# P.V, division and transposes of x of the first batch three steps, not five, behind a slot's mask

## The chip, the core and the metric

The kernel runs on one core of a Trainium2 chip. The metric is the time of one execution in microseconds (us) on the device; the median of several executions counts. The core's engines work in parallel, each through its own list of instructions in order: TensorE (PE) does matmuls and transposes and loads weights (PEld), VectorE (DVE), ScalarE (ACT) and GpSimd (POOL) work elementwise, and SyncE (SP) issues the DMAs of this kernel. Semaphores make an instruction wait for what it needs. [...]

## What is computed

Attention with a threshold over 4 batches, 8 heads, 576 positions and 64 dimensions a head; then two gated feed-forward layers over the 2304 tokens.

```python
scores = scale * np.matmul(q, k.transpose(0, 1, 3, 2))
thresh = np.max(scores, axis=-1, keepdims=True) - tau
scores = np.where(scores >= thresh, scores, -1000000000.0)
scores = scores - np.max(scores, axis=-1, keepdims=True)
attn = np.exp(scores)
attn = attn / (np.sum(attn, axis=-1, keepdims=True) + 1e-09)
return np.matmul(attn, v).astype(np.float32)
...
gate = 1.0 / (1.0 + np.exp(-(x @ w_gate)))
val = x @ w_val
return (gate * val @ w_out).astype(np.float32)      # layer one: 512 -> 1536 -> 512
...
a = x @ w1
b = x @ w2
h = a * b @ w3
return (h @ w_out).astype(np.float32)               # layer two: 512 -> 1024 -> 512
```

## The kernel before

**Attention.** Heads are taken in pairs: 16 pairs, four to a batch (`NPAIR` = 4). The queries of a pair fall into nine row blocks of 128, called slots (`NSL` = 9): four for each head, and one, the tail, that holds the last 64 rows of both. So there are `G` = 144 slots, 36 to a batch. Slot g passes through these steps:

- `s_mm` (PE): the score products into one of two PSUM buffers, `ps_s0` for even g and `ps_s1` for odd; products are split into a high and a low part, so that a slot takes two or three passes (`ka` and `ylz`, for the tail `xk` and `yk`);
- `s_max` (DVE, tile `nm`, line 321) and `s_exp` (ACT, tile `e`, line 327);
- `s_mask` (DVE, line 336): exponentials below the threshold become 0, and the row sum is taken. It frees the PSUM buffer for slot g+2;
- `s_hi` (ACT, line 344), and `s_lo` (ACT line 355 and POOL line 358, or DVE line 360): P as two 16-bit halves, tile `h16`, shown as `h`;
- `s_tr`: a transposing DMA, issued on SP (line 364), writes `pt`, of which there are five buffers;
- `pv` (PE): 14 small matmuls (28 for a tail) of `pt` with `vh`, `vl` and `vsh`, into `u`, and for the tail into a corner of a score buffer (`ut`).

After a pair's nine slots come `x_norm` (DVE: division by the row sums, tiles `xn` and `xt`), `x_pe` (PE: transposes, tiles `ps_x` and a corner of `ps_s`) and `x_act` (ACT, lines 417 and 419: into the x of the batch, `XR0` to `XR3`). A pair is a quarter of the 512 features of x, chunk c of four. The next pair's q, k and v are loaded, transposed, split and scaled meanwhile (`t_pe` to `v_split`, by the table `ahead`).

**Work between the slots.** `filler` puts other matmuls into the program twice a step. At first it is `merge_gen`, which multiplies w3 by w_out (tiles `woh`, `wol`); then `l1_gen`, layer one. Layer one runs batch by batch: an `h_unit` gives two units of 12 matmuls (`ps_h`, 288 columns), an `o_unit` nine (`ps_o`). It needs x of its batch split into high and low halves (`xh` on ACT, `xl` on POOL or DVE, line 467 and 468), chunk by chunk, and `ready(b)` holds it until `xdone` counts the batch. Its weights arrive by DMA and are cast and split for batch 0 on DVE, ACT and POOL (lines 449 to 468). `budget(g)` sets how much of it a call takes: until g = 44 one unit a call, later so much that the batches' work is spread evenly up to the time when the next batch is ready. Layer two follows all attention.

**Order.** The loop at line 825 runs over steps g and traces the parts in a fixed order: mask of g, maximum of g+1, scores of g+2, `s_tr` of g-2, and P.V of g-5 (`LAG` = 5); `x_norm` falls into step 9n+5, `x_pe` and `x_act` into the two after it. This order is only a priority: the scheduler takes, engine by engine, what is ready in its own reckoning of time. So the order of the built program differs from the order of the text.

```python
done = divmod(g - LAG, NSL)
...
if done[1] == 2 and done[0] > 0:
    x_act(done[0] - 1)
    if done[0] % NPAIR == 0:
        xdone[0] = done[0] // NPAIR
filler(g, 0)
...
if 0 <= g - LAG < G:
    pv(g - LAG, g)
```

Of the kernel before, what the change touches and what calls it, by code (L numbers as in the profile page):

```python
# [22 lines left out]
def kernel(  # L23
# [25 lines left out]
    NPAIR = H // 2  # L49
# [243 lines left out]
    NSL = 2 * NC + 1  # L293
# [91 lines left out]
    def x_norm(pr):  # L385
        p = prep[pr]
        rs = ap_.tile([P, NSL], F32, tag="rs", name="rs", bufs=1)
        nc.vector.tensor_scalar(rs, p["sum"], 1e-9, None, op0=ALU.add)
        nc.vector.reciprocal(rs, rs)
        xn = ap_.tile([P, NC, 2, D], F32, tag="xn", name="xn")  # L390
        xt = ap_.tile([P, 2, D], F32, tag="xt", name="xt")
        nc.vector.tensor_tensor(
            xn.rearrange("p c h d -> p h c d"), p["u"],
            rs[:, 0:2 * NC].rearrange("p (h c x) -> p h c x", h=2, x=1).to_broadcast([P, 2, NC, D]),
            op=ALU.mult,
        )
        nc.vector.tensor_scalar(
            xt, p["ut"][:, 0:P].rearrange("p (x d) -> p x d", x=2),
            rs[:, 2 * NC:NSL], None, op0=ALU.mult,
        )  # L400
        p.update(xn=xn, xt=xt)
# [77 lines left out]
    def flush(keep):  # L479
        while len(defer) > keep:  # L480
            defer.pop(0)()
# [257 lines left out]
    xdone = [0]  # L739
# [6 lines left out]
    LAG = 5  # L746
    G = NP * NSL
    spent = [0]

    def run(gen, ns):  # L750
        while gen is not None and ns > 0:
            t = next(gen, "end")
            flush(1)
            if t == "end":
                return None
            if t is None:
                return gen
            ns -= t
            spent[0] += t
        return gen  # L760
# [64 lines left out]
    for g in range(G + LAG + 3):  # L825
        pr, s = divmod(g, NSL)
        steps = ahead[s] if pr + 1 < NP else ([],) * 5
        done = divmod(g - LAG, NSL)
        if g < G:
            s_mask(g)  # L830
        if g + 1 < G:
            s_max(g + 1)
        if g < G:
            s_hi(g)
        if g + 1 < G:
            s_exp(g + 1)
        if g + 2 < G:
            s_mm(g + 2)
        for f in steps[3]:
            f(pr + 1, g)  # L840
        if done[1] == 0 and done[0] > 0:
            x_norm(done[0] - 1)
        if g < G and g % 2 == 0 or g // (NPAIR * NSL) == 0:
            s_lo(g)
        if 0 < g <= G and not ((g - 1) % 2 == 0 or (g - 1) // (NPAIR * NSL) == 0):
            s_lo(g - 1)
        if 2 <= g < G + 2:
            s_tr(g - 2)
        for f in steps[0]:
            f(pr + 1)  # L850
        for f in steps[1]:
            f(pr + 1)
        if done[1] == 2 and done[0] > 0:
            x_act(done[0] - 1)
            if done[0] % NPAIR == 0:
                xdone[0] = done[0] // NPAIR
        filler(g, 0)
        for f in steps[2]:
            if isinstance(f, str):
                if pr + 2 < NP:  # L860
                    load(src[f], pr + 2, f)
            else:
                f(pr + 1)
        if 0 <= g - LAG < G:
            pv(g - LAG, g)
        for f in steps[4]:
            f(pr + 1)
        if done[1] == 1 and done[0] > 0:
            x_pe(done[0] - 1, g)
        filler(g, 1)  # L870
    order.close()
    actx.close()
# [282 lines left out]
```

## Time and profile before

| | |
|---|---|
| Runs | 1141.19, 1147.88, 1150.70 us; median 1147.88 |
| The profiled execution | 1143.68 us, its span 1141.9 us |
| Busy, of the span | PE 90%, weight loads 85%, DVE 69%, POOL 58%, ACT 55% |
| Mean granted clock of PE | 0.965 |
| Matmuls | 8256 |
| DMA | 324738 packets, 245.34 MB |

A busy share is an average over stretches with different limits, so the views below are cut by stretch: 143 us is about the end of the merge, 209.5 us the place where layer one of batch 0 gets going, 353 us about slot 72, 392 us about slot 82, and 711 us the last P.V. The releaser in brackets is what ended the idle time of the engine ahead of the row. Helpers record several kinds of matmul under one line (63), so tiles tell them apart.

### The profile page before, as it was taken

The numbers are of one execution on the slowest core, as the hardware profiler recorded it, in microseconds if no ns is written. First come the engines' busy times: TensorE is split into PE (matmuls) and PEld (weight loads), VectorE is DVE, ScalarE is ACT, GpSimd is POOL, SyncE is SP. The second block draws the span as 40 slices with busy tenths as digits, with TensorE's granted clock in tenths as the row PEclk, the third lists the DMA queues.
The fourth block names the chain that finished last, engine by engine and source line by source line (L and its number), as shares of the span: only waits on it lengthen the run. The fifth ranks groups of instructions, "written<-read, shape, count | busy, mean of one in ns | idle before, by whom it ended". The sixth has DMA issues, their size and how long they took to land.

```text
span 1141.9 us, 23155 instructions
## 1 busy us (share of the span) xinstructions
PE 1024.9 (90%) x8256; PEld 967.5 (85%) x8256; DVE 788.6 (69%) x1485; ACT 626.1 (55%) x1306; POOL 657.9 (58%) x593
## 2 busy tenths in 40 slices
PE   2598956899898799999899999999789999999997
PEld 2477745799888799999799999989789989998996
DVE  6988588988797766677757754698886653662740
ACT  4877797878587666566656665545542311231210
POOL 2655384688685866766665685577862441460420
PEclk9999968899899899999899999999989999999999
DMA  7999999999998898977876764898767857866824
GB/s 211 260 277 208 221 214 176 268 272 264 275 259 211 193 209 177 182 172 174 183 178 148 159 142 113 292 371 298 257 202 232 253 174 228 266 194 188 289 77 129
DMA packets 324738, 245.34 MB, mean 215 GB/s; under 512 B 225552, under 2 KB 254224, under 8 KB 324624
## 3 DMA queue, kind: packets, MB, share of 16 engines
q1 hardware_dynamic: 324624, 243.87, 82.2%
q8 instruction: 65, 1.06, 0.4%
q14 instruction: 49, 0.40, 0.1%
HBM read 141.56 MB, written 35.13 MB: 155 GB/s over the span
## 4 chain that ended last, share of the span: by engine, by line
PE 60%; DMA 13%; DVE 10%; POOL 5%; issue 5%; ACT 4%; SPq 3%; DVEq 0%; POOLq 0%; ACTq 0%
PE ps_h L63 16%; PE ps_ab L63 15%; PE ps_o L63 9%; PE ps_y L63 8%; PE ps_s L63 6%; DMA pt<-h 4%; PE u L63 3%; DMA vnat<-in_v_dram 1%; PE ps L63 1%; DMA sc_c<-wc 1%; DVE e L336 1%; DVE ps_c L449 1%; DVE nm L321 1%; DMA XR<-in_moe_w_out_dram 1%; DMA wms<-sc_m 1%
## 5 line engine op out<-in xcount | busy, mean ns | idle before, releaser
L358 POOL TENSOR_TENSOR h<-e,h 128x576 f16<-128x576 f32 x90 | 117.0, 1302 | 50.8 <-ACT e L355 35.0
L327 ACT ACTIVATE e<-ps_s,nm 128x576 f32<-128x576 f32 x144 | 106.2, 738 | 59.8 <-DVE nm L321 57.5
L63 PEld LDWEIGHTS <-pt 128*128 128x128 f16 x2240 | 83.7, 102 | 61.8 <-DMA pt<-h 50.2
L321 DVE TENSOR_REDUCE nm<-ps_s 128x1 f32<-128x576 f32 x144 | 107.2, 751 | 40.1 <-PE ps_s L63 26.9
L63 PE MATMUL ps_o<-gvl,oh 128*128 128x288 f32 x384 | 118.8, 312 | 9.5 <-DVE XR L695 5.6
L63 PE MATMUL ps_h<-xl,gh 128*128 128x288 f32 x384 | 120.9, 315 | 6.6 <-ACT gh L467 4.4
L336 DVE SCALAR_TENSOR_TENSOR e<-ps_s,th,e 128x576 f32<-128x576 f32 x144 | 116.8, 812 | 14.1 <-ACT th L328 10.3
L63 PE MATMUL ps_h<-xl,vh 128*128 128x288 f32 x384 | 117.6, 306 | 3.5 <-ACT th L664 1.8
L63 PE MATMUL ps_h<-xh,gl 128*128 128x288 f32 x384 | 115.4, 300 | 4.6 <-DVE gl L468 4.6
L63 PE MATMUL ps_o<-gvh,ol 128*128 128x288 f32 x384 | 114.8, 299 | 0.5 <-DVE ol L468 0.5
L63 PE MATMUL ps_h<-xh,vl 128*128 128x288 f32 x384 | 114.8, 299 | 0.4 <-DVE vl L468 0.4
L63 PE MATMUL ps_h<-xh,gh 128*128 128x288 f32 x384 | 114.9, 299 | 0.0
L63 PE MATMUL ps_o<-gvh,oh 128*128 128x288 f32 x384 | 114.3, 299 | 0.0
L344 ACT ACTIVATE h<-e 128x576 f16<-128x576 f32 x144 | 97.3, 678 | 30.9 <-DVE e L336 25.5
L63 PE MATMUL ps_h<-xh,vh 128*128 128x288 f32 x384 | 114.2, 298 | 0.0
L63 PE MATMUL u<-vh,pt 128*128 128x64 f16 x640 | 63.6, 201 | 45.2 <-DMA pt<-h 44.4
L468 POOL TENSOR_TENSOR gvl<-gr,gvh 128x288 fp32r<-128x288 f32 x82 | 74.0, 902 | 47.1 <-ACT gvh L467 42.3
L63 PE MATMUL ps_y<-wm,abh 128*128 128x512 f32 x288 | 91.7, 391 | 0.2 <-DMA wm<-sc_n 0.2
L63 PE MATMUL ps_s<-ka,qa 128*128 128x288 f32 x256 | 64.4, 339 | 27.4 <-DVE e L336 15.4
L1023 POOL TENSOR_TENSOR v<-u,u 128x384 f32<-128x384 f32 x24 | 25.5, 1068 | 107.7 <-DVE u L1023 56.6
L63 PEld LDWEIGHTS ps_o<-gvl,oh 128*128 128x128 f32 x384 | 73.7, 193 | 11.2 <-DVE XR L695 6.1
L669 DVE SCALAR_TENSOR_TENSOR gr<-th,ps_h 128x288 f32<-128x288 f32 x96 | 43.2, 450 | 56.2 <-PE ps_h L63 34.8
(199 smaller groups left out, 3284.5 us busy)
## 6 DMA issues: line engine op xcount, KB each, us to landing
wc<-sc_c SPq DMA_DIRECT2D x168, 256.0 KB, 3.3
sc_c<-wc SPq DMA_DIRECT2D x56, 256.0 KB, 4.6
wm<-sc_n SPq DMA_DIRECT2D x24, 512.0 KB, 3.5
XR<-in_moe_w_out_dram SPq DMA_DIRECT2D x20, 512.0 KB, 4.8
ka<-xk SPq DMA_DIRECT2D x64, 144.0 KB, 3.3
wg<-sc_g SPq DMA_DIRECT2D x36, 256.0 KB, 3.5
wv<-sc_v SPq DMA_DIRECT2D x36, 256.0 KB, 3.2
wo<-sc_o SPq DMA_DIRECT2D x36, 256.0 KB, 3.5
```

Of the source, the lines that this page charges most:

```text
L63: nc.tensor.matmul(out_, lhsT, rhs, start=first, stop=last)
L321: nc.vector.tensor_reduce(nm, x["ps"], axis=AX.X, op=ALU.max, negate=True)
L327: nc.scalar.activation(e, x["ps"], AF.Exp, bias=x["nm"])
L336: nc.vector.scalar_tensor_tensor(x["e"], x["ps"], x["th"], x["e"], op0=ALU.is_ge, op1=ALU.mult, accum_out=prep[pr]["sum"][:, s:s + 1],)
L344: nc.scalar.activation(x["h16"][:, 0:S], x["e"], AF.Copy, scale=PSC)
L358: nc.gpsimd.tensor_tensor(lo, e, hi, op=ALU.subtract)
L449: first = nc.vector.tensor_scalar(t0, hw, 3, 0xC0000000, op0=ALU.logical_shift_left, op1=ALU.bitwise_or)
L468: (lo_eng or nc.gpsimd).tensor_tensor(lo, x, hi.bitcast(F32), op=ALU.subtract)
L669: nc.vector.scalar_tensor_tensor(r, t, 1.0, pss["v"][:, 0:HS], op0=ALU.add, op1=ALU.mult)
L1023: eng.tensor_tensor(sv[w][nm], x, y, op=ALU.add)
```

## The change

A function `lag(g)` gives three for the slots of the first batch and five for the others. A step now takes P.V of each slot whose lag ends with it: step 38 takes that of slot 35, steps 39 and 40 none, step 41 that of slot 36. `x_norm`, `x_pe` and `x_act` come one, two and three steps behind the P.V of a pair's last slot; for batch 0 they move two steps ahead, and `xdone` becomes 1 at step 41 and no longer at step 43.

```diff
--- before.py
+++ after.py
@@ -747,6 +747,10 @@
     G = NP * NSL
     spent = [0]
 
+    def lag(g):
+
+        return LAG - 2 if g < NPAIR * NSL else LAG
+
     def run(gen, ns):
         while gen is not None and ns > 0:
             t = next(gen, "end")
@@ -825,7 +829,8 @@
     for g in range(G + LAG + 3):
         pr, s = divmod(g, NSL)
         steps = ahead[s] if pr + 1 < NP else ([],) * 5
-        done = divmod(g - LAG, NSL)
+        due = [x for x in range(max(0, g - LAG), min(g, G)) if x + lag(x) == g]
+        past = {g - x - lag(x): x // NSL for x in range(NSL - 1, min(g, G), NSL)}
         if g < G:
             s_mask(g)
         if g + 1 < G:
@@ -838,8 +843,8 @@
             s_mm(g + 2)
         for f in steps[3]:
             f(pr + 1, g)
-        if done[1] == 0 and done[0] > 0:
-            x_norm(done[0] - 1)
+        if 1 in past:
+            x_norm(past[1])
         if g < G and g % 2 == 0 or g // (NPAIR * NSL) == 0:
             s_lo(g)
         if 0 < g <= G and not ((g - 1) % 2 == 0 or (g - 1) // (NPAIR * NSL) == 0):
@@ -850,10 +855,10 @@
             f(pr + 1)
         for f in steps[1]:
             f(pr + 1)
-        if done[1] == 2 and done[0] > 0:
-            x_act(done[0] - 1)
-            if done[0] % NPAIR == 0:
-                xdone[0] = done[0] // NPAIR
+        if 3 in past:
+            x_act(past[3])
+            if past[3] % NPAIR == NPAIR - 1:
+                xdone[0] = past[3] // NPAIR + 1
         filler(g, 0)
         for f in steps[2]:
             if isinstance(f, str):
@@ -861,12 +866,12 @@
                     load(src[f], pr + 2, f)
             else:
                 f(pr + 1)
-        if 0 <= g - LAG < G:
-            pv(g - LAG, g)
+        for x in due:
+            pv(x, g)
         for f in steps[4]:
             f(pr + 1)
-        if done[1] == 1 and done[0] > 0:
-            x_pe(done[0] - 1, g)
+        if 2 in past:
+            x_pe(past[2], g)
         filler(g, 1)
     order.close()
     actx.close()
```

The names below are those of the two built programs, cut by lines left out. On ACT, at the end of batch 0's x: `XR_78` is x of batch 0, L419 the copy of the tail of its last pair, L327 and L328 the exponential and threshold of slots 43 and 44 (before) and 42 and 43 (after). Before:

```order
L327 ACTIVATE e<-ps_s_92,nm 128x576
L328 ACTIVATE th<-nm,ntau 128x1
L327 ACTIVATE e<-ps_s_91,nm 128x576
L328 ACTIVATE th<-nm,ntau 128x1
L419 ACTIVATE XR_78<-ps_s_91,vi 64x64 x2
L284 ACTIVATE vh<-vnat 128x640
L467 ACTIVATE xh<-XR_78 128x576
L344 ACTIVATE h_2649<-e 128x576
```

After:

```order
L327 ACTIVATE e<-ps_s_91,nm 128x576
L328 ACTIVATE th<-nm,ntau 128x1
L419 ACTIVATE XR_78<-ps_s_91,vi 64x64 x2
L327 ACTIVATE e<-ps_s_92,nm 128x576
L467 ACTIVATE xh<-XR_78 128x576
L328 ACTIVATE th<-nm,ntau 128x1
L344 ACTIVATE h_2671<-e 128x576
L284 ACTIVATE vh<-vnat 128x640
```

The copy stood behind the exponential of slot 44 and stands behind that of slot 42 now; the split of the last chunk (`xh`) follows one exponential later, ahead of `vh`.

On PE, where layer one of batch 0 goes on with the last chunk (`ps_h`): `xk,qbd` and `yk,qbd` are the scores of slot 44, `ka` and `ylz` those of the slots behind it, `u<-..,pt` rows P.V. Before:

```order
L63 MATMUL ps_s_91<-xk,qbd_93 128x288 x4
L63 MATMUL ps_s_91<-yk,qbd_93 128x288 x2
L411 MATMUL ps_s_91<-ident,xt 128x128
...
L63 MATMUL u<-vh,pt 128x64
...
L63 MATMUL ps_s_92<-ka,qa 128x288 x2
L63 MATMUL ps_s_92<-ylz_98,qa 128x288 x2
...
L63 MATMUL ps_s_91<-ka,qa 128x288 x2
L63 MATMUL ps_s_91<-ylz_98,qa 128x288 x2
...
L63 MATMUL u<-vsh,pt 128x64
L63 MATMUL ps_h<-xl,gh 128x288
L63 MATMUL ps_h<-xh,gl 128x288
```

After:

```order
L63 MATMUL ps_s_91<-xk,qbd_93 128x288 x4
L63 MATMUL ps_s_91<-yk,qbd_93 128x288 x2
L63 MATMUL ps_h<-xl,gh 128x288
L63 MATMUL ps_h<-xh,gl 128x288
L63 MATMUL ps_h<-xh,gh 128x288
L63 MATMUL ps_h<-xl,vh 128x288
L63 MATMUL ps_h<-xh,vl 128x288
L63 MATMUL ps_h<-xh,vh 128x288
L63 MATMUL ps_s_92<-ka,qa 128x288 x2
L63 MATMUL ps_s_92<-ylz_98,qa 128x288 x2
```

P.V of slots 39 to 41 and the scores of slots 45 and 46 stood between slot 44's scores and layer one; now layer one follows slot 44's scores at once.

On PE, at the scores of slot 34 (`ps_s_91<-ka` and `ylz_99`) and P.V of slot 29 (`u<-vh,pt` to `u<-vsh,pt`). Before:

```order
L63 MATMUL ps_s_91<-ka,qa 128x288 x2
L63 MATMUL ps_s_91<-ylz_99,qa 128x288 x2
L156 MATMUL ps_t<-ident,km 128x128 x4
L63 LDWEIGHTS vb
L63 MATMUL ps_s_91<-identb,vb 128x128
L63 LDWEIGHTS pt
L63 MATMUL u<-vh,pt 128x64
```

After:

```order
L411 MATMUL ps_s_92<-ident,xt 128x128
L63 LDWEIGHTS pt
L63 MATMUL u<-vh,pt 128x64
...
L63 MATMUL u<-vsh,pt 128x64
L63 MATMUL ps_s_91<-ka,qa 128x288 x2
L63 MATMUL ps_s_91<-ylz_99,qa 128x288 x2
```

The P.V stood behind the scores, and stands ahead of them now.

## Rows read from the trace of the kernel before

**Rows 1.** Page: the span of the profiled execution

```profile
span 1141.9 us, 23155 instructions
```

**Rows 2.** Busy time of each engine by stretch; first line names the columns

```profile
core 0: us, PE busy (x) PEld busy (x) DVE busy (x) ACT busy (x) POOL busy (x), PEclk, DMA share, GB/s
...
143.00:199.30 56.30, 32.77 (x351) 28.01 (x352) 45.82 (x99) 48.63 (x99) 37.41 (x31) 0.76 0.95 194
199.30:209.50 10.20, 7.09 (x62) 6.41 (x61) 8.27 (x15) 7.57 (x16) 3.11 (x4) 0.50 0.99 191
209.50:353.00 143.50, 133.39 (x1247) 128.50 (x1247) 125.37 (x246) 106.04 (x221) 112.64 (x96) 0.98 1.10 266
353.00:392.00 39.00, 30.77 (x313) 29.20 (x312) 29.04 (x60) 28.29 (x63) 29.55 (x26) 0.91 0.89 208
392.00:711.00 319.00, 312.77 (x3106) 303.70 (x3105) 211.33 (x431) 197.28 (x420) 209.65 (x197) 0.98 0.76 168
```

**Rows 3.** The same for line 336 alone (masks, two records a slot)

```profile
162.00:199.30 37.30, 11.51 (x28) 0.82 0.94 174
...
209.50:353.00 143.50, 22.13 (x54) 0.98 1.10 266
353.00:392.00 39.00, 8.28 (x21) 0.91 0.89 208
```

**Rows 4.** Timeline of PE (start us, us, instruction, idle before it), 199 to 213

```profile
199.63 1.16 PE L63 MATMUL ps_s<-xk,qbd 128*128 128x288 f32 x4
...
204.70 0.23 PE L63 MATMUL u<-vh,pt 128*128 128x64 f16 x1 [3.11 <-DMA pt<-h]
...
209.22 0.51 PE L63 MATMUL ps_h<-xl,gh 128*128 128x288 f32 x1
...
211.28 0.29 PE L63 MATMUL ps_h<-xh,gl 128*128 128x288 f32 x1
...
212.61 0.29 PE L63 MATMUL ps_h<-xh,gh 128*128 128x288 f32 x1
```

**Rows 5.** Timeline of ACT, same columns, 202 to 206

```profile
202.43 0.74 ACT L327 ACTIVATE e<-ps_s,nm 128x576 f32<-128x576 f32 x1 [1.75 <-DVE nm L321]
...
204.06 0.62 ACT L419 ACTIVATE XR<-ps_s,vi 64x64 f32<-64x64 f32 x2
...
205.34 0.67 ACT L467 ACTIVATE xh<-XR 128x576 fp32r<-128x576 f32 x1
```

**Rows 6.** Timeline of DVE, same columns, 203 to 208

```profile
203.20 0.82 DVE L279 TENSOR_TENSOR vnat<-vnat,ps_s 128x640 f32<-128x640 f32 x1
...
207.46 0.75 DVE L468 TENSOR_TENSOR xl<-XR,xh 128x576 fp32r<-128x576 f32 x1
```

**Rows 7.** Waits of PE, 209.5 to 353: who for whom, us, times, longest

```profile
PE ps_o L63 <- DVE XR L695: 5.6, 3, 3.9
PE ps_h L63 <- ACT th L664: 1.8, 2, 1.2
```

**Rows 8.** Waits of PE, 353 to 392

```profile
PE u L63 <- DMA pt<-h: 4.3, 1, 4.3
```

**Rows 9.** Timeline of PE, three pairs of score product and P.V

```profile
97.12 0.77 PE L63 MATMUL ps_s<-xk,qbd 128*128 128x288 f32 x4
...
99.16 0.19 PE L63 MATMUL u<-vh,pt 128*128 128x64 f16 x1
...
171.94 0.52 PE L63 MATMUL ps_s<-ka,qa 128*128 128x288 f32 x2
...
174.09 0.20 PE L63 MATMUL u<-vh,pt 128*128 128x64 f16 x1 [0.87 <-DMA pt<-h]
...
176.53 0.54 PE L63 MATMUL ps_s<-ka,qa 128*128 128x288 f32 x2
...
177.95 0.20 PE L63 MATMUL u<-vh,pt 128*128 128x64 f16 x1 [0.62 <-DMA pt<-h]
```

**Rows 10.** Waits of PE, 60 to 209.5

```profile
PE u L63 <- DMA pt<-h: 24.1, 15, 3.1
```

## Prediction

> **What bounds the kernel now.** I read the table of busy time by stretch first, because the share of the whole span hides that the stretches have different limits. From 392 us to 711 us PE is busy for 312.77 of 319 us, and from 209.5 to 353 us for 133.39 of 143.5 us; from 143 to 199.3 us it is busy for only 32.77 of 56.3 us, at a granted clock of 0.76 [rows 2]. So from 209.5 us the kernel is a stream of matmuls with attention threaded through it, and ahead of that it is attention by itself, waiting on chains between engines. I then read the pace of attention from the masks alone: 14 slots in 37.3 us (2.66 us each) from 162 to 199.3 us, where PE has little besides attention; 27 slots in 143.5 us (5.3 us each) where layer one of batch 0 fills PE; and 10.5 slots in 39 us (3.7 us each) from 353 to 392 us, where that work runs out ahead of batch 1's [rows 3]. The waits of the first stretch say what PE waits for there: 15 times for the transposed P to land, 24.1 us in all [rows 10].
>
> The point where the first stretch turns into the second is layer one of batch 0 getting its last quarter of x. The first 18 matmuls ran early on the other three quarters; the rest resumes at 209.22 us [rows 4], 0.3 us ahead of the clock's rise from 0.50 at 209.5 us [rows 2]. That is the place the change touches most.
>
> **The change part by part.** Nothing is added or removed: as many matmuls, divisions, copies and DMAs as before. P.V, division and transposes of x of slots 0 to 35 are traced two steps earlier, and batch 0 counts as done at step 41, not 43. The scheduler then orders the engines anew.
>
> P.V itself hardly moves. In the order of PE I counted how many slots' scores stand ahead of each P.V: for slots 8 to 38 it is slot plus 4.5 on average in both kernels. Its readiness, not its place in the program, set its position already. Single ones move: those of slots 12, 29 and 31 now stand ahead of a score product that used to precede them. By the times of before, PE would be held from 97.12 to 99.16, from 171.94 to 174.09 and from 176.53 to 177.95 us [rows 9]: 2.0, 2.2 and 1.4, in sum 5.6 us at most. Others (13, 14, 21 to 24) move the other way. At least nothing is lost, since PE has 23.5 us of idle time there from 143 to 199.3 us [rows 2]; I take a quarter, **+1.3 us**, nearer to that idle time. If that cover is gone, all 5.6 us count. Behind a waiting P.V on PE stands the next score product, and for that wait the maximum, the exponential and the mask of its slot.
>
> The end of x moves. Now: the copy of the tail of x at 204.06, the split's high half at 205.34 [rows 5], its low half from 207.46 to 208.21 [rows 6], then P.V of slots 39 to 41 and two scores, then layer one at 209.22 [rows 4]. After: on ACT the copy stands ahead of slot 43's exponential and the high half right behind it. That exponential ran at 202.43 for 0.74 us [rows 5], so the high half ends about 203.9; the low half stands behind the product on `vnat`, which ends at 204.02 [rows 6], and ends about 204.8. On PE the resumed matmuls now stand right behind slot 44's scores (199.63 [rows 4]) and ahead of P.V 39. So layer one resumes at about 204.8, 4.4 us earlier. What is that worth? Not the 3.11 us in which PE waited for P.V 39 until 204.70 [rows 4]: the new first instruction is ready no sooner. What remains is that PE worked at half clock until 209.5 [rows 2]. If the clock rises with layer one, as it did at 209.5, the 4.7 us from 204.8 hold 2.4 us more work; if it does not, nothing. I take **-2.4 us**, the row's own coincidence.
>
> The rest of layer one's work is shifted, not shortened. A matmul of 288 columns takes (212.61-211.28)/10 = 0.133 us [rows 4]; two steps with two filler calls each give four units of 12, or 6.4 us of PE earlier. In the new order 396 of layer one's matmuls stand ahead of slot 58's scores, where 312 stood; 756 ahead of slot 72's, where 708 stood; and 819 ahead of slot 81's in both, since batch 1 still becomes ready at step 79. The lead is given back. So two slots without layer one leave the first stretch and two join the stretch from 353 us. Out go 2 x 2.66 = 5.3 us, in come 2 x 2.66 to 2 x 3.7 = 7.4 us: 0 to +2.1 us. I take **+1.0 us**, the middle, since the slots at 3.7 us carried layer one's remainder.
>
> Last, layer one's own waits. Spread over two more slots, its accumulations into x (5.6 us of waiting in 3 places) and its tanh (1.8 us) may be awaited less [rows 7]. Bounds 0 and -7.4 us; I take **-3.0 us**, under half, because the order of DVE that makes the longest (3.9 us) is not undone. The DMA queue of SP issues the same transfers; its transposes stand within two or three rows of where they stood, so I cost them at nothing, hidden by the 5.3 us a slot has in that stretch; without that cover the price is one more wait as that of 4.3 us [rows 8].
>
> Sum: +1.3 - 2.4 + 1.0 - 3.0 = -3.1 us. The profiled execution took 1143.68 us (span 1141.9 [rows 1] and 1.8 us around it); it would become 1140.6. The median of the runs is 4.2 us above it, 1147.88, and becomes 1144.8, or 1145 in round figures.
>
> **The rivals.** *Nothing moves.* P.V keeps its distance, layer one is level at slot 81, and PE is full from there; the four terms cancel. For it speaks that the order of PE is nearly the same from about slot 86 on; against it, the half clock just ahead of 209.5. Time: 1147.9.
>
> *The lead is kept.* If attention, rid of layer one in the stretch from 353 us, runs its slots there at 2.66 us as it did ahead of 199.3, two slots (5.3 us) are saved outright, with the 2.4 us of clock and the 7.4 us of waits: -15.1 us, 1132.8. For it: that pace was reached once [rows 3]. Against: PE waited 4.3 us there for one P.V [rows 8], so latency and not PE held it. It decides from about 12 us in all.
>
> *P.V holds back the scores.* A P.V on PE that comes two steps sooner waits for its transposed P, and the next scores wait behind it; then batch 0 slows down. One wait costs 24.1/15 = 1.6 us [rows 10]; from eight more such waits (12.8 us) the kernel is slower by over 1%, about 1160.5. For it: three such pairs are in the order. Against: three make 5.6 us, not 12.8, and the mean distance is unchanged. [...]
>
> **How the numbers follow.** Chances: my forecast 0.46, nothing moves 0.25, the lead kept 0.17, P.V holding back 0.12. About 1% is what a measurement of this kernel can tell from no change: 1136.4 to 1159.4 us. The forecast's own bounds are -2.4-7.4 = -9.8 (1138) and +5.6+2.1 = +7.7 (1155.6). With half of the two outer rivals taken in, the range is 1134 to 1156. Faster by over 1%: 0.18, the kept lead and a trace of the forecast; slower: 0.11; within 1%: 0.71.
>
> **What would show it.** In the profile of the changed kernel: the first resumed `ps_h` matmul ahead of P.V 39, some 4 us before the same slot's place now; the clock at 1.00 a few us sooner after it; 5 us a slot or more while layer one runs; a longer stretch of slots at 3 to 3.7 us ahead of 392 us. PE's waits for the landing of transposed P up to 209.5 us should stay near 24 us. If they pass 36 us, I am wrong on the slow side; if the stretch ahead of slot 83 runs at 2.7 us a slot, on the fast side. A shift of the whole profile after 711 us would be none of these.

## The result, and the profile after

The changed kernel takes 1153.85 us (median of 16 runs, 1146.35 to 1159.07), the kernel before on the same chip 1146.92 us (16 runs, 1141.19 to 1152.58). The ratio is 1.0065, interval 1.0045 to 1.0085: **7 us slower**, where 3 us faster was forecast. The profiled execution of the changed kernel is the fastest of all its runs (1146.35 us), so that the readings below are repeated on two more profiles of each order of instructions.

Its span on the page:

```profile
span 1144.6 us, 23156 instructions
```

The same table by stretch as [rows 2] (PE, PEld, DVE, ACT, POOL busy, granted clock, DMA share, GB/s), cut where the clock rises. The granted clock is TensorE's, as a share of full; the clock records of both kernels' profiles hold only 1.00 and 0.50 (half), and a stretch shows the mean:

```profile
143.00:196.50 53.50, 31.46 (x313) 26.79 (x313) 43.49 (x84) 44.12 (x89) 35.86 (x31) 0.68 0.93 189
196.50:209.50 13.00, 10.42 (x108) 9.76 (x108) 11.59 (x27) 11.13 (x26) 4.86 (x5) 1.00 0.88 202
209.50:353.00 143.50, 137.18 (x1321) 131.68 (x1320) 126.98 (x251) 108.19 (x225) 113.15 (x98) 1.00 1.12 266
353.00:392.00 39.00, 26.90 (x261) 23.78 (x260) 29.41 (x56) 27.27 (x57) 28.94 (x25) 0.82 0.99 211
392.00:711.00 319.00, 308.89 (x3040) 299.56 (x3040) 210.59 (x428) 194.50 (x416) 205.78 (x193) 0.98 0.77 169
```

Against [rows 2], PE does more from 209.5 to 353 us (137.18 us busy for 133.39), and less in the two stretches behind: 26.90 for 30.77, and 308.89 for 312.77. The masks of line 336 (two records a slot; answers to [rows 3]) tell the same of attention:

```profile
162.00:199.30 37.30, 9.40 (x23) 0.72 0.90 173
209.50:353.00 143.50, 22.73 (x56) 1.00 1.12 266
353.00:392.00 39.00, 8.13 (x20) 0.82 0.99 211
```

The timeline of PE where layer one resumes, answering [rows 4]; P.V of slot 39 now stands behind it:

```profile
205.39 0.40 PE L63 MATMUL ps_h<-xl,gh 128*128 128x288 f32 x1 [0.34 <-DVE xl L468]
...
210.01 0.21 PE L63 MATMUL u<-vh,pt 128*128 128x64 f16 x1
```

And the waits of PE (who for whom, us, times, longest): from 60 to 209.5 us (answers [rows 10]), from 209.5 to 353 (the four longest; [rows 7]), from 353 to 395 ([rows 8]) and from 395 to 545 us:

```profile
PE u L63 <- DMA pt<-h: 21.4, 13, 3.9
...
PE ps_x L407 <- DVE XR L693: 1.6, 1, 1.6
PE ps_h L63 <- DVE yk L239: 1.1, 1, 1.1
PE ps_h L63 <- ACT vh L467: 1.0, 1, 1.0
PE ps_s L63 <- DVE e L336: 0.9, 1, 0.9
...
PE ps_s L63 <- DVE e L336: 9.2, 4, 5.1
...
PE ps_o L63 <- DVE XR L693: 2.2, 1, 2.2
PE ps_h L63 <- DVE XR L695: 1.6, 1, 1.6
```

In the kernel before, the masks from 353 to 395 us:

```profile
PE ps_s L63 <- DVE e L336: 3.7, 3, 1.6
```

So the waits for transposed P did not grow, of the 5.6 us for accumulations into x 0.4 us are left, and two new ones stand further down: 9.2 us for masks where 3.7 stood, and 2.2 us for a copy into x in a place where the kernel before waits for nothing.

**Where the time goes, stretch by stretch.** Stretches cut by the clock on the wall compare different work, so I cut by work. Each matmul counts with the median interval from its start to the next one's, over those at full clock with no idle time between (by its operands, from the profiles of both kernels). Both kernels then hold the same 952.4 us of work, and a mark says how much of it PE has begun. The table gives the time between marks, mean and range over three profiles: of the kernel before (first profile, before_again, before_red) and of the changed one (first profile, after_again, after_red). Early marks cut off slightly different sets of matmuls; behind 262 the orders of PE differ by some dozens of rows, and from mark 308 (445 to 449 us) on the list of every engine is the same in both kernels.

| Work marks | time in before | before, us | changed, us | difference |
|---|---|---|---|---|
| 0 to 90 | to 172 | 168.8 (167.0 to 172.0) | 167.0 (166.3 to 167.5) | -1.8 |
| 90 to 120 | to 225 | 53.9 (53.1 to 55.1) | 50.4 (49.8 to 50.9) | -3.5 |
| 120 to 240 | to 362 | 136.2 (135.7 to 136.9) | 133.4 (132.8 to 134.5) | -2.7 |
| 240 to 262 | to 397 | 36.0 (35.0 to 36.5) | 42.3 (42.0 to 42.7) | +6.3 |
| 262 to 400 | to 541 | 143.8 (142.4 to 144.7) | 150.1 (148.4 to 153.3) | +6.3 |
| 400 to 430 | to 583 | 40.3 (38.6 to 41.3) | 42.0 (41.3 to 42.9) | +1.6 |
| 430 to end | to 1134 | 551.2 (550.6 to 551.7) | 551.6 (549.8 to 553.0) | +0.4 |

The sum is +6.7 us, close to what the medians say; the three profiles of the changed kernel by themselves give +1.5, +7.2 and +11.3. So 8.0 us are won up to mark 240, and 14.2 lost from there to 430. From 90 to 262, where layer one of batch 0 runs, win and loss cancel.

### The profile page after: what moved, and what is told of

It is laid out like the page before. It is cut to its first block, busy times and chain, and to the rows that moved or that the text cites. A ratio compares the mean times of both kernels' runs of the same rounds, so it can differ in the third digit from the quotient of the medians.

```text
span 1144.6 us, 23156 instructions
## 1 busy us (share of the span) xinstructions
PE 1026.5 (90%) x8256; PEld 965.8 (84%) x8256; DVE 790.5 (69%) x1485; ACT 625.7 (55%) x1306; POOL 657.4 (57%) x593
## 4 chain that ended last, share of the span: by engine, by line
PE 58%; DVE 14%; DMA 11%; ACT 6%; issue 6%; POOL 4%; SPq 1%; DVEq 0%; POOLq 0%; ACTq 0%
PE ps_h L63 16%; PE ps_ab L63 15%; PE ps_y L63 8%; PE ps_o L63 7%; PE ps_s L63 5%; DMA pt<-h 4%; PE ps L63 3%; PE u L63 3%; DVE ps_c L449 2%; DVE nm L321 2%; DVE e L336 2%; DVE t L455 1%; ACT h L344 1%; DMA wms<-sc_m 1%; DMA vnat<-in_v_dram 1%
## 5 line engine op out<-in xcount | busy, mean ns | idle before, releaser
L327 ACT ACTIVATE e<-ps_s,nm 128x576 f32<-128x576 f32 x144 | 106.5, 739 | 57.0 <-DVE nm L321 52.9
L321 DVE TENSOR_REDUCE nm<-ps_s 128x1 f32<-128x576 f32 x144 | 107.5, 751 | 40.3 <-PE ps_s L63 23.7
L336 DVE SCALAR_TENSOR_TENSOR e<-ps_s,th,e 128x576 f32<-128x576 f32 x144 | 116.6, 812 | 15.4 <-ACT th L328 11.5
L63 PEld LDWEIGHTS ps_h<-xl,gh 128*128 128x128 f32 x384 | 73.8, 192 | 12.1 <-ACT gh L467 4.9
L468 POOL TENSOR_TENSOR ol<-wo,oh 128x512 fp32r<-128x512 f32 x41 | 56.7, 1390 | 45.4 <-ACT oh L467 45.4
```

The lines of the kernel that those rows point to most:

```text
L63: nc.tensor.matmul(out_, lhsT, rhs, start=first, stop=last)
L321: nc.vector.tensor_reduce(nm, x["ps"], axis=AX.X, op=ALU.max, negate=True)
L327: nc.scalar.activation(e, x["ps"], AF.Exp, bias=x["nm"])
L336: nc.vector.scalar_tensor_tensor(x["e"], x["ps"], x["th"], x["e"], op0=ALU.is_ge, op1=ALU.mult, accum_out=prep[pr]["sum"][:, s:s + 1],)
L468: (lo_eng or nc.gpsimd).tensor_tensor(lo, x, hi.bitcast(F32), op=ALU.subtract)
```

## The experiments

All ratios are to the kernel before, on the same chip in the same session (its medians there 1145.0 to 1146.2 us). The right half is the table above for the one profile of each run: difference to the mean of the kernel before, by stretch and in sum, in us.

| Run | ratio, 95% interval | 0-90 | 90-120 | 120-240 | 240-262 | 262-400 | 400-430 | rest | sum |
|---|---|---|---|---|---|---|---|---|---|
| last_pair | 1.0010 (0.9986 to 1.0035) | +0.8 | -2.8 | -2.5 | +6.3 | +0.8 | -0.8 | -0.5 | +1.3 |
| first_pairs | 1.0089 (1.0061 to 1.0116) | -1.2 | +2.4 | +3.7 | +2.4 | +2.8 | -0.3 | -1.4 | +8.4 |
| two3 | 0.9990 (0.9971 to 1.0009) | -3.0 | -1.8 | -3.6 | +3.0 | +7.3 | -0.9 | +0.9 | +2.1 |
| after_again | 1.0065 (1.0041 to 1.0089) | -2.6 | -3.3 | -1.7 | +6.8 | +4.8 | +1.4 | +1.8 | +7.2 |
| before_again | 1.0008 (0.9987 to 1.0028) | +3.2 | -0.4 | -0.5 | +0.5 | +0.9 | +0.8 | +0.5 | +5.1 |
| before_spread8 | 0.9981 (0.9963 to 1.0000) | +0.3 | -0.8 | +6.0 | -6.3 | +0.3 | -4.9 | +2.8 | -2.6 |
| after_spread8 | 0.9987 (0.9971 to 1.0004) | +0.3 | -3.1 | +13.0 | -3.5 | +0.3 | -5.6 | -3.2 | -1.9 |
| after_spread4 | 1.0097 (1.0072 to 1.0123) | -0.7 | -3.3 | +5.2 | +2.1 | +2.3 | -3.0 | +14.8 | +17.4 |
| last_pair_spread8 | 1.0015 (0.9993 to 1.0036) | +1.1 | -4.3 | +11.5 | -6.0 | +1.0 | -4.3 | +4.3 | +3.3 |
| two3_spread8 | 0.9987 (0.9970 to 1.0005) | -1.3 | -2.8 | +4.0 | -6.6 | +3.6 | -0.3 | +1.3 | -2.0 |
| vmax_dep0 | 1.0047 (1.0021 to 1.0074) | -0.4 | -4.2 | -2.6 | +6.1 | +3.5 | +2.0 | +0.5 | +4.9 |
| late_start | 1.0068 (1.0046 to 1.0090) | +2.7 | -0.2 | +3.2 | -1.4 | +1.7 | -0.4 | +0.5 | +6.1 |
| hold_start | 1.0129 (1.0107 to 1.0152) | -0.6 | -1.6 | +6.1 | +1.4 | +0.5 | +2.9 | 0.0 | +8.7 |
| pair0 | 1.0107 (1.0085 to 1.0129) | -2.6 | +0.2 | +11.1 | +2.7 | -1.5 | +0.5 | +0.9 | +11.4 |
| after_red | 1.0066 (1.0041 to 1.0092) | -1.4 | -3.0 | -3.4 | +6.2 | +9.6 | +2.5 | +0.9 | +11.3 |
| hold_start_red | 1.0069 (1.0046 to 1.0093) | +1.9 | -1.5 | +5.4 | +2.0 | +1.4 | +0.5 | +0.5 | +10.2 |
| before_red | 1.0001 (0.9981 to 1.0021) | -1.3 | +1.2 | -0.2 | +0.5 | -1.4 | -1.7 | -0.7 | -3.7 |
| after_spread8_red | 0.9995 (0.9972 to 1.0017) | -1.6 | -4.3 | +13.8 | -1.7 | -0.1 | -6.9 | -3.5 | -4.4 |

The profiled execution can stand up to 7.5 us beside its kernel's median (the first of the changed kernel; those of first_pairs and hold_start are the fastest of their six runs, that of after_spread4 the slowest), so the sums on the right do not follow the ratios closely. Between marks 90 and 430 the three profiles of one order agree within 3 us in each stretch, but for 262 to 400 in after_red; ahead of 90 they differ by up to 5 us, behind 430 by up to 3.2.

**Which part of the change.** One edit of `lag` each:

```
last_pair    return {31: 4, 32: 4, 33: 3, 34: 3, 35: 3}.get(g, LAG)
first_pairs  return LAG - 2 if g < (NPAIR - 1) * NSL else LAG
two3         return LAG - 2 if g < 2 * NPAIR * NSL else LAG
```

> Only the last pair of batch 0 catches up: P.V keeps five steps up to slot 30, four for slots 31 and 32, three for 33 to 35, so that batch 0 counts as done at step 41 as in the changed kernel, while PE's order of P.V against scores up to slot 36 is that of the kernel before. Layer one's lead on PE is there: 384 of its matmuls ahead of slot 58's scores (changed kernel 396, before 312). Theory L (the time is lost because layer one's lead takes work away from the slots ahead of 392 us, where attention then runs by itself): slower than before by the whole 5 to 7 us, ratio 1.004 to 1.007, and the PE wait on masks from 353 to 395 us near 9 us, as in the changed kernel, against 3.7 before. Theory P (the P.V that stand ahead of scores up to slot 36 hold attention back): no change, ratio 0.998 to 1.002. If the loss is from both, 1.002 to 1.004.

> Only slots 0 to 26 have P.V three steps behind; the last pair has five again, so batch 0 counts as done at step 43 as before. PE's order of P.V against scores is that of the changed kernel up to slot 34, and layer one stands as before (300 matmuls ahead of slot 58's scores, before 312). Theory L: no change, ratio 0.998 to 1.002, attention in the stretch from 353 us as before. Theory P: the whole loss, ratio 1.004 to 1.007, with slot 40's mask 4 to 5 us late as in the changed kernel.

> Three steps for batches 0 and 1, so that batch 1 too counts as done two steps earlier; on PE 858 of layer one's matmuls stand ahead of slot 82's scores where both other kernels have 819, so layer one of batch 1 begins inside the stretch that had run out of it. Theory L: the stretch from 353 to 395 us gets its filler back; PE's wait on masks there falls from 9.2 us to 4 us or less and the time to that of before or below: ratio 0.995 to 1.001. Theory P: the loss stays, ratio 1.004 to 1.007, as it lies in batch 0.

> The changed kernel once more, beside the three others on one chip, for a second profile and the spread of its granted clock. Its profiled run was the fastest of its 16 (1146.35 us at a mean clock of 0.966; the median 1153.85). If the loss of the typical run lies where the profiled run shows it (353 to 395 us and 395 to 482 us), the second profile shows the same stretches longer and the rest alike; if it lies in the clock, half-clock stretches stand in other places than before, such as after 711 us. Ratio 1.0045 to 1.0085 again by either.

Theory L fell as it was put: the early start alone (last_pair) costs nothing that can be measured. But its stretches show both halves: 5.3 us won from mark 90 to 240, 6.3 us lost from 240 to 262. There PE waits for masks 7.2 us (L expected near 9, against 3.7 before), and it is the early start and not P.V that does it, since P.V stands as before up to slot 36:

```profile
PE ps_s L63 <- DVE e L336: 7.2, 3, 4.0
PE u L63 <- DMA pt<-h: 1.3, 1, 1.3
```

first_pairs lost even more than P expected, 1.0089, but not by P's means: P.V waits 21.5 us for transposed P up to 209.5 us there, no more than before [rows 10], slot 40's mask is 1.9 us late and not 4 to 5 (the profiles of the kernel before differ by 5 us there), and what is lost lies in layer one's stretches. two3 came out at L's number, and by L's place in part: the waits for masks from 353 to 395 us fall from 9.2 to 5.3 us, and the stretch from 240 to 262 by 3.3 us, but from 262 to 400 it loses as much as the changed kernel. after_again gave 1.0065 once more, its profile 6 us above the first; 3.2 of them lie behind mark 430, the rest is spread.

**Is the lead lost because layer one runs out?** The spread kernels let layer one of a batch run eight (or four) steps longer:

```
-  return (e * L1_NS - spent[0]) / (2 * ((e + 1) * n + LAG + 3 - g)) if e else 1.0
+  return (e * L1_NS - spent[0]) / (2 * ((e + 1) * n + LAG + 11 - g)) if e else 1.0
```

> The changed kernel, with layer one of each batch spread over eight more steps (to step 88 for batch 0, where it ended at 80). Its start and the whole order up to slot 52 stay those of the changed kernel (180 of its matmuls ahead of slot 52's scores in both), but it no longer runs out: 660 matmuls stand ahead of slot 72's scores, where 756 stood, and 492 ahead of slot 64's, where 540 stood. Theory R (the changed kernel gains 5 to 7 us from the earlier start and pays 7 us for it where layer one runs out ahead of 395 us, and 4 us behind): the idle time and half clock of that stretch shrink to 6 us or less, the start's gain remains, ratio to the kernel before 0.994 to 1.000. Theory P (P.V's order against the scores in the first three pairs is what costs, as first_pairs at 1.0089 speaks for): the loss stays, some 6 to 8 us above before_spread8, ratio 1.002 to 1.008.

> The kernel before with the same eight steps more for layer one: 624 of its matmuls ahead of slot 72's scores where 708 stood, and from slot 82 the order of the changed kernel with this edit (819, 852 to 858, 924, 984 ahead of slots 82, 84, 86, 88). Theory R: attention ahead of 392 us is fed here too, 3 to 6 us less, ratio 0.994 to 0.999; and the changed kernel with the edit lies within 2 us of this one, or below it, since its earlier start is kept. Theory P: it gains the same 3 to 6 us, but the changed kernel with the edit stays 6 to 8 us above it.

> As after_spread8 with four steps more, to step 84: 708 of layer one's matmuls ahead of slot 72's scores, which is what the kernel before has, though the start and the order of P.V are the changed kernel's. So the lead is given back between slots 64 and 72 and not where layer one runs out. Theory R: the stretch from 353 to 395 us as before (8 us idle), ratio 0.997 to 1.002. Theory P: ratio 1.004 to 1.008.

> The kernel before, once more, for a second profile and as a measure of the comparison itself: ratio 1.000 with 0.998 to 1.002 about it. Its granted clock in the first profile was 0.965, that of the median run about 0.963. If the stages by which I compare the profiles are steady from run to run, then the time in which PE does the same amount of work differs by no more than 1.5 us from the first profile in each stage from 209 to 711 us; stages that differ by more cannot carry an argument from a single profile.

> P.V as before up to slot 30, batch 0 done at step 41 (last_pair), and layer one spread over eight more steps. Layer one has 156 matmuls ahead of slot 52's scores (before_spread8 120) and 660 ahead of slot 72's (624). If the early start is worth 5 us wherever it is not given back: 4 to 5 us below before_spread8 (1142.63), some 1138, ratio 0.992 to 0.995. If what it wins goes into other waits of the mixed stretch, as in after_spread8 where PE was idle 17.5 us there: level with before_spread8 or above it, ratio 0.997 to 1.002.

> P.V three steps behind in batches 0 and 1, and layer one spread over eight more steps: the start two steps sooner in both batches, with the order of P.V in the first pairs that the changed kernel has. Layer one has 201 matmuls ahead of slot 52's scores and 847 ahead of slot 82's (before_spread8 120 and 819). If the order of P.V in the first pairs costs by itself: 4 to 8 us above last_pair_spread8. If it does not and the starts are worth their lead: level with last_pair_spread8 or below it, ratio 0.990 to 0.995.

With eight steps both of R's ratios came out, and the stretch from 240 to 262 did as R says: it shrinks by 6 to 12 us against the same kernel without the spread. But R's reason does not carry the ratio. From mark 90 to 262 after_spread8 takes 232.4 us where the changed kernel takes 226.1, since the stretch from 120 to 240 grows by more than the next one shrinks; what it wins lies behind mark 262, where R names 4 us at most: 6.0 us from 262 to 400, 7.2 from 400 to 430 (where the clock is never at half, against 10.2 us of it in the changed kernel) and 3.6 behind. Why the spread brings that about stays open. The early start's win goes into another place too: last_pair_spread8 has 3.5 us less than before_spread8 from mark 90 to 120 and 5.5 us more (11.5 against 6.0) from 120 to 240, and its ratio is higher by 0.0034 (by one profile of each, in two sessions). In the five kernels whose P.V stand as before (the kernel before, last_pair, late_start, before_spread8, last_pair_spread8) the time from mark 90 to 262 is 226.1, 227.1, 227.6, 225.0 and 227.2 us. So as long as P.V stands as before, attention up to slot 83 with layer one of batch 0 takes some 226 us, however the second is laid into the first. With P.V three steps behind it is not so fixed: 226.1 us in the changed kernel, 223.9 in two3, 220.7 in two3_spread8 and 232.4 in after_spread8. two3_spread8 starts layer one as early as last_pair_spread8 and gives nothing back there, so that the early start is not a zero sum in every layout. The order of P.V by itself, the last question, costs nothing that shows: two3_spread8 (0.9987) was to be 4 to 8 us above last_pair_spread8 (1.0015) if it did, and is level with it within the intervals; the 0.990 to 0.995 of the other theory did not come either, and its second batch differs too. after_spread4 missed both theories; its loss lies at the end (mark 430 on: +14.8), and its cause is open. None of these beats the kernel before by more than its interval; before_spread8, after_spread8 and two3_spread8 beat the changed one by 9 to 10 us, by their ratios. before_again stands within some 1.5 us of the first profile in every stretch from mark 90 to 430, and not ahead of it.

The mask that PE waits for longest in the changed kernel's lost stretch shows what that time is. From the timelines of DVE, ACT, DVE (two rows) and PE:

```profile
357.88 1.68 DVE L360 SCALAR_TENSOR_TENSOR h<-e,h 128x576 f16<-128x576 f32 x1
...
359.60 0.74 ACT L327 ACTIVATE e<-ps_s,nm 128x576 f32<-128x576 f32 x1
...
361.00 0.23 DVE L187 TENSOR_TENSOR yk<-ps_s,xk 128x64 fp32r<-128x64 f32 x1 [1.43 <-ACT qbd L180]
...
361.74 0.82 DVE L336 SCALAR_TENSOR_TENSOR e<-ps_s,th,e 128x576 f32<-128x576 f32 x1
...
362.62 1.59 PE L63 MATMUL ps_s<-ka,qa 128*128 128x288 f32 x4 [5.05 <-DVE e L336]
```

The exponential starts 0.04 us after the end of `s_lo` on DVE, which the profile gives as its releaser, then come the mask and the scores. It is mostly attention's own chain. But this `s_lo` took 1.68 us where 0.7 is its shortest (the last part of this section shows beside what such cases stand), and the mask does not follow the exponential at once: that ends at 360.34, and in DVE's list two steps of the next pair stand ahead of the mask, for which DVE waits 1.43 us. PE has no layer one to put under all this: from slot 74's scores to slot 77's its list holds none (780 of layer one's matmuls stand ahead of both), where in the kernel before it holds 36 (744 and 780).

**The second loss, and the start.**

```
vmax_dep0    if pr == 11:      # in v_max, ahead of the maximum
                 nc.vector.tensor_reduce(vm[:, 0, 0:1], prep[10]["sum"][:, 0:1], axis=AX.X, op=ALU.max)
hold_start   xdone[0] = 1 at step 43 instead of 41, P.V as in the changed kernel
late_start   xdone[0] = 1 at step 45 instead of 43, else the kernel before
pair0        return LAG - 2 if g < NSL else LAG
```

> The changed kernel with one added reduction of 128x1 on DVE, by which the maximum over V of pair 11 comes behind the mask of slot 90; the order of ACT, POOL and SP is the changed kernel's row for row, and DVE's but for this one place, where the maximum now stands behind the copies into x of layer one as in the kernel before. Theory D (part of the loss is that this maximum, which waits for V to land, stands ahead of the copies that PE waits for: 2.2 us of PE idle at 442.80 us in both profiles of the changed kernel, none in both of the kernel before): that idle time is gone, the stretch from 395 to 482 us 2 to 4 us shorter, ratio to the kernel before 1.003 to 1.005 where the changed kernel has 1.0065. Rival: the time is given back within the next slots since attention is late there anyway: ratio 1.005 to 1.008 as the changed kernel.

> The changed kernel with P.V three steps behind in batch 0, but batch 0 counts as done at step 43, as before. PE's order of P.V against scores up to slot 38 is the changed kernel's; layer one has 336 matmuls ahead of slot 58's scores (changed 396, before 312), and the maximum of pair 11 stands behind the copies into x as before. Theory L (layer one's early start is what costs): ratio 0.999 to 1.002. Theory P (P.V's order in the first pairs costs, and the early start hides part of it, as first_pairs at 1.0089 against 1.0065 speaks for): 1.006 to 1.010, with the loss ahead of 260 us.

> The kernel before with batch 0 counted as done at step 45, two steps later: layer one has 288 matmuls ahead of slot 58's scores where 312 stood, and 696 ahead of slot 72's where 708 stood; P.V's order up to slot 41 is that of before. On DVE the maximum of pair 11 stands ahead of the copies into x, as in the changed kernel. If the start of layer one is a zero sum (what is won by an early one is given back where layer one runs out, as last_pair at 1.001 speaks for), a late one is too: 2 to 4 us lost ahead of 260 us, 3 to 6 us won from 353 to 395 us. With the 2 to 4 us of the maximum's place the ratio is 1.000 to 1.004, and 2 us or more of PE idle stand near 443 us. If an early start were worth its lead, 1.004 to 1.008.

> Only the first pair (slots 0 to 8) has P.V three steps behind. In the order of PE the P.V of slots 8 to 38 then stand behind slot plus 5.2 scores on average (before 4.5, changed 4.5), so they come later and not sooner; layer one 300 to 312 matmuls ahead of slot 58's scores as before. Theory P in its narrow form (P.V that come too soon hold back scores): no loss, ratio 0.998 to 1.002. Theory N (any edit up there makes the scheduler lay the engines out anew, and what is lost or won follows the new layout, not the distance of P.V): a change of either sign and up to 10 us, 0.995 to 1.010, with idle times of PE at other places than in both kernels.

In the changed kernel DVE has, from mark 300 on, `rs`, then the maximum over V, which waits for V to land, then a mask, the reciprocal and an `s_lo`, and only then three copies into x (timelines of DVE and, last line, PE):

```profile
436.83 0.45 DVE L693 TENSOR_SCALAR XR<-ps_o 128x288 f32<-128x288 f32 x1
437.20 1.51 DVE L388 TENSOR_SCALAR rs<-sum 128x9 f32<-128x9 f32 x1
439.63 1.28 DVE L245 TENSOR_REDUCE vm<-vnat 128x128 bf16<-128x640 f32 x1 [0.92 <-DMA vnat<-in_v_dram]
...
442.29 1.18 DVE L693 TENSOR_SCALAR XR<-ps_o 128x288 f32<-128x288 f32 x3
...
442.80 0.40 PE L63 MATMUL ps_o<-gvl,oh 128*128 128x288 f32 x1 [2.21 <-DVE XR L693]
```

In the kernel before, a copy stands ahead of that maximum, with others following as PE needs them (timeline of DVE):

```profile
436.45 0.44 DVE L693 TENSOR_SCALAR XR<-ps_o 128x288 f32<-128x288 f32 x1
438.08 1.31 DVE L245 TENSOR_REDUCE vm<-vnat 128x128 bf16<-128x640 f32 x1 [1.19 <-DMA vnat<-in_v_dram]
```

vmax_dep0 puts it back (line 247 is the maximum, 695 the copy):

```profile
442.52 0.45 DVE L695 TENSOR_SCALAR XR<-ps_o 128x288 f32<-128x288 f32 x1
...
442.95 0.44 DVE L695 TENSOR_SCALAR XR<-ps_o 128x288 f32<-128x288 f32 x1
443.32 1.32 DVE L247 TENSOR_REDUCE vm<-vnat 128x128 bf16<-128x640 f32 x1
```

PE's 2.2 us are gone, so the wait is what theory D says. The ten units of work around the place took 14.0 us in the changed kernel (mean of three), 10.5 in the kernel before and 10.7 here, so 3.5 of the 6.3 us are this one wait with the half clock that follows it in two of three profiles. What that is worth in the whole is less sure: the ratio falls from 1.0065 to 1.0047, 2 us, which is in D's range, but its interval (1.0021 to 1.0074) holds the rival's too, and the stretch from 262 to 400 keeps +3.5 us in its one profile. late_start, where the same order stands on DVE without the change, has the wait too: 2.6 us.

late_start's ratio, 1.0068, is that of a start worth its lead, and its profile does not bear that out: from mark 90 to 262 it is 1.6 us above the kernel before, the wait near 443 us brings 2.8, and the rest stands ahead of mark 90, where nothing was edited. It decides nothing. hold_start and pair0 were worse than any theory, though they change less. pair0 speaks against P in its narrow form: P.V comes later there, and the loss is larger, just above N's upper edge. The part of their loss that their one profile shows (8.7 of some 15 us in hold_start, 11.4 of 12 in pair0) lies mostly from 120 to 240, where PE is idle 15.7 us in pair0 and 12.0 in hold_start, against 8.7 in the kernel before and 6.4 in the changed one (means of three), most of it behind layer one's copies into x and accumulations. So without the early start a new order of the first pairs costs 4 to 11 us there (first_pairs, hold_start, pair0); with it, in the changed kernel, none.

**What makes those waits.** In seven of the profiles a small instruction on DVE, the addition ahead of the division's reciprocal, lasts 3 to 5 us in places, and in some of them PE waits behind it, so I replaced it:

```
-  nc.vector.tensor_scalar(rs, p["sum"], 1e-9, None, op0=ALU.add)
+  nc.vector.tensor_reduce(rs, p["sum"].rearrange("p (n x) -> p n x", x=1), axis=AX.X, op=ALU.max)
```

> The changed kernel with the addition in front of the division's reciprocal replaced by a reduction of one element each (it leaves out the 1e-9 that is added to the sums). Order of all engines as in the changed kernel. Theory S (that addition is held back while POOL works, in some runs by some us, and the copies into x wait behind it): 3 to 6 us below the changed kernel, ratio to the kernel before 1.001 to 1.004, and the reduction takes 0.2 us or less in all 16 pairs. Rival (what it is held back is hidden): 1.0055 to 1.0075 as the changed kernel.

> hold_start (1.0129) with the same replacement. Its profile had the addition at 296 us for 4.13 us, and PE idle for 3.61 us at 301.6 us behind it. Theory S: that idle time is gone and the ratio is 1.008 to 1.010. Rival: 1.011 to 1.015.

> The kernel before with the same replacement. From 209 to 435 us its addition took 0.16 to 0.59 us in both profiles, so there is nothing to win there; ahead and behind it took 1.0 to 1.2 us in six or seven pairs, where attention has little beside it. Theory S: ratio 0.998 to 1.001. If the 1 us stalls of the attention-only stretches are on the path too: 0.994 to 0.997.

> after_spread8 (0.9987) with the same replacement. Its profile had the addition at 346 us for 5.23 us and PE idle for 4.40 us at 352.1 us behind it. Theory S: 3 to 5 us faster, ratio 0.994 to 0.997, below both the kernel before and the changed one. Rival: 0.997 to 1.000.

Theory S fell for the changed kernel: 1.0066, no change. before_red (1.0001) came out as S has it, where there was nothing to win. after_spread8 did not gain either (0.9995, the rival's range), and its two profiles say why. With the addition (timelines of DVE, POOL, the first and last of the five in a row beside it, and PE):

```profile
345.69 5.23 DVE L388 TENSOR_SCALAR rs<-sum 128x9 f32<-128x9 f32 x1
...
345.14 1.31 POOL L458 TENSOR_TENSOR wo<-t,t 128x512 int32<-128x512 int32 x1
...
349.62 1.27 POOL L468 TENSOR_TENSOR gl<-wg,gh 128x512 fp32r<-128x512 f32 x1
...
352.07 0.40 PE L63 MATMUL ps_o<-gvl,oh 128*128 128x288 f32 x1 [4.40 <-DVE XR L695]
```

Without it the next instruction on DVE, `s_lo`, takes its place in the wait:

```profile
343.51 0.16 DVE L388 TENSOR_REDUCE rs<-sum 128x9 f32<-128x9 f32 x1
343.60 5.40 DVE L360 SCALAR_TENSOR_TENSOR h<-e,h 128x576 f16<-128x576 f32 x1
...
349.49 0.40 PE L63 MATMUL ps_o<-gvl,oh 128*128 128x288 f32 x1 [4.01 <-DVE XR L697]
```

The addition ended at 350.92, 0.03 us after POOL's fifth instruction. `s_lo` on DVE (0.7 us at its shortest, 0.9 to 1.0 in the median) ends 0.60 to 0.62 us after an instruction of POOL ends in all its cases above 1 us. hold_start_red did fall, from 1.0129 to 1.0069, but its profile has `s_lo` at 299.8 for 4.66 us instead and PE idle for 3.56 us behind it, so where the 5 to 7 us between the two (by medians or by ratios) went stays open: below S's range, and not by S's means.

## Why the prediction was right or wrong

**P.V ahead of scores (+1.3).** A quarter of 5.6 is 1.4, and the first of the three places, at 97 us, stands ahead of the stretch whose idle time was to cover it; neither matters. Right that nothing much is paid: up to mark 90 the changed kernel is 1.8 us ahead, within the 5 us by which the profiles of the kernel before differ there, and P.V waits 21.4 us for transposed P, where the bound for being wrong was 36. In the built program, tracing P.V of slot 4, 12 or 20 alone one step sooner leaves every engine's list row for row as it was: its place in the trace does not set its place there. PE still stands idle where a P.V waits, 21.4 us in 13 places where 24.1 us in 15 stood; only no more of them wait.

**The start of layer one (-2.4).** Right in place and near in size: it resumes at 205.39 us, forecast 204.8, and 3.5 us are won from mark 90 to 120. The reason was wrong. The clock had been at 1.00 from 196.5 us (second row of the table by stretch), 8.9 us before layer one resumed, and in before_red it rose at 209.6, 0.3 us ahead of it; the rise that coincided with it in [rows 2, 4] was not its doing. What set off the earlier rise stays open.

**Layer one's own waits (-3.0).** Right in size, 2.7 us from 120 to 240, and wrong in one clause, that the order behind the 3.9 us wait is not undone. It is. In the kernel before that wait is `s_lo` on DVE behind a row of POOL's (timelines of DVE, POOL and PE):

```profile
291.11 4.57 DVE L360 SCALAR_TENSOR_TENSOR h<-e,h 128x576 f16<-128x576 f32 x1
...
293.80 1.27 POOL L358 TENSOR_TENSOR h<-e,h 128x576 f16<-128x576 f32 x1
...
296.10 0.61 PE L63 MATMUL ps_o<-gvl,oh 128*128 128x288 f32 x1 [3.93 <-DVE XR L695]
```

In the changed kernel the longest cases of this line in that stretch are 3.07 and 2.63 us; PE waits 1.6 us behind the first (`ps_x` in the waits above) and not at all behind the other.

**The lead is given back (+1.0, bounds 0 to +2.1).** The mechanism was right and the size wrong: +6.3 us. The step that failed here is "two slots without layer one leave the first stretch and two join": I priced the move by the difference of two paces, 2.66 and 3.7 us a slot [rows 3]. Measured, the slots of that stretch run at 3.9 us (10 in 39 us), and what counts is not their pace but that PE stands still under them: 12.0 us idle against 8.0 (means of three profiles, marks 240 to 262), and the clock at half for 13.6 to 17 us against 6.8 to 10.2. Half of the lead's 11 us (84 matmuls at slot 58 by 0.133) was lost again where it ended.

**What was not in the sum at all (0).** This is the other step that failed, and it cost more. From the words that the order of PE is nearly the same from slot 86 on I took it that nothing changes there; 7.9 us (6.3 and 1.6) are lost behind mark 262. PE's order is nearly the same, DVE's is not, and for 3.5 of these us PE waits for DVE (vmax_dep0). The 1.6 us from 400 to 430 are no wait for DVE: the lists are the same there, and the clock is at half for 10.2 us in all three profiles of the changed kernel and for 10.2, 3.4 and 0 us in those of the kernel before. The other 2.8 us are spread in small pieces and stay open. The transfers of SP cost PE nothing at first hand, as forecast (from 353 to 395 us it waited 0.9 us for transposed P, where 4.3 stood in [rows 8]); at second hand they did, through the maximum that waits for V. Why some edits of the first pairs cost 10 to 15 us (by their ratios) is shown only as far as the waits go; which row of which engine brings them about for each is open.

In sum: -8.0 us where -4.1 was forecast for the same three terms, +6.3 for +1.0, +7.9 for nothing. The time, 1153.85, lies in the stated range and within 1%, but on the other side of the kernel before; that it lies so near is luck, since 8.0 us of wins and 14.2 of losses stand behind it, neither of which was forecast in its size. Neither outer rival did it: P.V does not wait longer than before, and the lead is not kept.

## What to carry to other kernels

Work that fills the gaps of a chain may be worth nothing earlier if the chain then runs without it: price the place where the filler runs out, by PE's idle time there, and not by the pace of the stretches. Where a scheduler lays out every engine anew, compare the order of all engines down to the end, not only that of the busiest one, and look for instructions that wait for a transfer with something behind them that the busy engine needs. Marks of equal work, over two or three profiles, find such losses where stretches of equal time hide them.

## What the runs showed of the hardware

Two instructions on DVE lasted in places until a whole row of POOL's instructions had ended: the 128x9 addition took 0.16 us alone (at 295.97 us in the kernel before) and 5.23 us beside five in a row (after_spread8), `s_lo` 0.7 us at its shortest and 5.40 us in after_spread8_red. The record of that addition begins at 345.69 us, ahead of four of the five, and ends behind all of them. All of the longer cases end a fixed time behind an instruction of POOL: 0.03 to 0.04 us for the addition and 0.60 to 0.62 for `s_lo` (in the profiles of the kernel before and of the changed one 22 additions above 0.3 us and 52 `s_lo` above 1 us). The reduction that replaced the addition took 0.15 to 0.17 us in all 64 cases of four profiles. What ties these two to POOL, and why the reduction was not held, no run shows.
